# Two attentions in one kernel: the order of all steps and the choice of engines set anew

## The chip, the cores and the metric

The kernel runs on one core of a Trainium2 chip. The metric is the device time in microseconds (us) of one execution. The engines are TensorE (PE), VectorE (DVE), ScalarE (ACT), GpSimd (POOL) and SyncE (SP, which issues the DMAs here). TensorE's results land in PSUM; the other operands lie in SBUF.

## The reference

`B, H, S, D = 8, 8, 576, 64`. A first attention has two parts whose outputs are added; a mixture of four causal attention heads works on the sum.

```python
q_d = q.reshape(B, H, Sd, 4, D).mean(axis=3)          # k_d, v_d likewise; Sd = 144
out_d = sm_attn(q_d, k_d, v_d)                        # softmax attention on pooled rows
out_up = np.repeat(out_d, 4, axis=2)
mask = np.abs(pos[:, None] - pos[None, :]) < 4
out_local = softmax(np.where(mask, q @ k.T / 8, -1e9)) @ v
x = (out_up + out_local) as [B, S, H * D]

logits = x @ w_gate                                   # 4 experts, the best 2 by softmax weights
for e in range(4):
    a = causal_softmax((x @ wq[e]) @ (x @ wk[e]).T / 8)
    out += gate[e] * (a @ (x @ wv[e]) @ wo[e])
```

## The kernel before

The work is cut by batch (8) and, in the first attention, by pair of heads (4 pairs, index `c`); in the second by pair of experts (index `p`, 2) and by unit of query blocks (`u`, 1 to 4). Three stages overlap: while stage 3 of batch `b` runs, stage 2 of `b + 1` and stage 1 of `b + 2` run beside it.

- Stage 1, `s1_local`: scores of a band of 64 columns, mask (`l_mask`, L500), maximum (`l_max`, L503), subtraction (`l_sub`, L512), exponent (`l_exp`), sum (`l_sum`, L515), `l_rec`, and the norm `l_nrm` (L518). `s1_down`: q, k and v pooled by four (`qd` and `kd`; `vd`, two additions L549 and L550 on `lr` and `vd`), scores, exponent (`d_exp`), norm `d_nrm` (L591, on ACT three instructions of L589). `s1_out`: transposes, products, the sum `x` (L652), and its split into a rounded part `xh` (L657, ACT) and a rest `xl` (L658), with a short rest `xt` (L660), since the projections multiply in a rounded float32 and correct with the rest.
- Stage 2: projections `qk` and `v` (L681), a tail `vt`, the gate.
- Stage 3: `s2_scores` (L821) with mask and maximum (`s_max`, L841), exponent on ACT (`s_exp`, L844), sum (`s_eps`, L314 on POOL), reciprocal (`s_rec`, L849), and the norm `s_nrm` (L852), which multiplies the rows `pr` by reciprocal and gate weight; `s2_trans` transposes the rows (`tq`); `s2_av` multiplies with v, adds the two halves (`o_add`), and splits the result into `oh` (L942, ACT) and the rest `ol` (`o_lo`, L943); `s2_out` multiplies with `wo` and stores.

Every step is written as a call of `op(kind, engines, cost, function, ...)`. Where two engines are named, either can run it:

```python
op("s_nrm", "GV", (...), lambda g, ...: eng[g].tensor_scalar(
    rows_of[t], rows_of[t], st[:, x, 3:4], gt()[:, t, p:p + 1], op0=OP.mult, op1=OP.mult), ...)
op("o_lo", "GV", (...), lambda g: eng[g].tensor_tensor(
    ol()[:, qlo:qhi], o()[:, 0:n], oh()[:, qlo:qhi].bitcast(F32), op=OP.subtract), ...)
```

The steps are not emitted in the order in which they are written. The table `SEQ` holds one number for each: the step's index times four, plus which of its engines runs it (or, for `down`, which of two row halves comes first); -1 is a filler matmul that keeps PE busy. `schedule` reads it, and each engine runs its instructions in that order:

```python
for x in SEQ:
    o = self.ops[x // 4] if x >= 0 else self.filler()
    o.which = x % 4 if x >= 0 else 0
    o.who = o.eng[o.which]
    out.append(o)
```

An engine waits, by semaphores, for the data of its next instruction, and what stands behind that one in its queue waits too. Nothing in the program orders DVE against POOL where they share no data. The four PSUM buffers (`big`) are handed out in the order of `SEQ` as well.

Of the kernel before, what the change touches and what calls it, by code (L numbers as in the profile page):

```python
# [17 lines left out]
    24, 4, 177, 0, -1, -1, -1, -1, 136, 173, 124, 120, 140, 189, 192, 197, 144, 272, 200, -1, 232, 16, 216, 236, 149,  # L18
    268, -1, -1, -1, 284, 152, 8, 220, 240, 205, 12, 412, 208, 416, 288, 244, 376, 156, 360, 160, 214, 164, 248, 364,
    380, 180, 168, 320, 185, 293, 324, 532, 296, 384, 429, 252, 432, 568, 312, 256, 224, 504, 536, 437, 316, 388, 508,  # L20
    776, 572, 736, 228, 328, 332, 260, 300, 265, 540, 304, 708, 128, 336, 308, 392, 396, 440, 456, 340, 420, 544, 460,
    772, 816, 712, 444, 548, 400, 344, 740, 404, 584, 464, 424, 784, 840, 368, 132, 408, 468, 588, 612, 448, 592, 596,
    276, 744, 748, 28, 453, 552, 788, 600, 616, 844, 904, 604, 752, 900, 372, 348, 512, 793, 988, 609, 556, 280, 756,
    620, 472, 760, 353, 560, 357, 796, 624, 992, 476, 480, 668, 672, 32, 913, 916, 1056, 484, 764, 564, 921, 488, 37,
    812, 768, 924, 492, 500, 628, 632, 636, 640, 576, 580, 660, 20, 940, 800, 1016, 1052, 497, 804, 64, 664, 944, 644,
    648, 656, 1196, 676, 1020, 1200, 680, 1065, 684, 40, 45, 688, 876, 728, 520, 68, 652, 810, 92, 84, 48, 1172, 724,
    1068, 928, 692, 100, 720, 716, 516, 848, 1204, 1236, 696, 56, 880, 52, 1024, 61, 705, 1209, 524, 1168, 781, 104,
    528, 76, 820, 112, 948, 1073, 1076, 853, 73, 1212, 884, 952, 824, 1444, 700, 1232, 932, 888, 1028, 1244, 896, 956,
    80, 892, 1216, 1248, 960, 1081, 1508, 1084, 1221, 964, 968, 938, 1252, 856, 1032, 89, 972, 860, 1224, 1140, 1144,
    1100, 96, 864, 976, 985, 868, 1088, 1104, 1148, 732, 1440, 1280, 1036, 873, 981, 909, 828, 1284, 1504, 1152, 1320,  # L30
    1256, 1092, 1761, 1156, 1324, 1260, 1161, 1517, 1328, 1060, 1041, 1096, 1544, 1468, 1044, 1520, 1264, 1556, 1564,
    1548, 1764, 1048, 1228, 1525, 1004, 1528, 1108, 996, 1472, 1112, 1116, 1120, 1124, 1533, 1188, 1476, 1680, 1268,
    1368, 1536, 1540, 1272, 1332, 1336, 1340, 1684, 1372, 1552, 1276, 1480, 1344, 1836, 1376, 1840, 1484, 1192, 1988,
    2404, 1348, 1560, 1688, 832, 1000, 1241, 1568, 1693, 1696, 1488, 1656, 1773, 1352, 1776, 1492, 836, 1724, 1380,
    2072, 1728, 1652, 1736, 1700, 1288, 1496, 1984, 1128, 1356, 1704, 1137, 1180, 1781, 1292, 1296, 1784, 1388, 1384,
    1132, 1788, 1300, 1360, 1792, 1304, 1400, 1404, 1392, 1397, 1452, 1364, 1740, 2356, 2360, 1732, 1876, 1176, 1888,
    1500, 1828, 1832, 2068, 1008, 1448, 2080, 1184, 1880, 2084, 2012, 1592, 1308, 2016, 1596, 1012, 1408, 1412, 1416,
    2089, 2092, 2328, 2400, 1745, 1604, 1708, 1573, 1576, 1748, 2413, 1312, 1892, 1600, 2020, 1317, 2844, 1420, 1424,
    2416, 1628, 1796, 2024, 1712, 1632, 2144, 2149, 1428, 2028, 2421, 2032, 1588, 2848, 1884, 1757, 1896, 1752, 2332,
    1672, 1585, 1581, 1432, 1608, 1900, 1612, 1636, 2036, 1616, 1512, 1620, 1624, 1640, 1716, 1676, 2424, 1905, 1668,  # L40
    2429, 1844, 1908, 2364, 1437, 1664, 1644, 1720, 1848, 1852, 1800, 1648, 2368, 1804, 2136, 1912, 1856, 2097, 2040,
    1860, 2140, 1976, 1980, 1968, 2940, 1972, 1917, 2872, 2044, 2100, 2876, 1456, 2372, 2106, 1164, 1808, 1460, 2376,
    2432, 2292, 2304, 3648, 2296, 2880, 2936, 2381, 1812, 1660, 2048, 2052, 2184, 2308, 1864, 2056, 2524, 1816, 2196,
    2188, 2456, 1873, 1768, 116, 2460, 1868, 1920, 2436, 2384, 1940, 2388, 1464, 1924, 3004, 2528, 1996, 1932, 2884,
    2200, 1820, 2060, 2192, 1928, 3008, 1824, 2532, 2076, 2228, 2152, 2156, 2160, 2240, 2205, 2244, 2232, 2300, 2236,
    1992, 2976, 2108, 2464, 2112, 2116, 2000, 2164, 3012, 2168, 2469, 2120, 1944, 3016, 2208, 2172, 2249, 2620, 2409,
    1936, 1948, 1952, 2625, 3080, 2216, 2472, 2476, 2004, 2348, 2480, 2212, 2180, 2176, 2628, 2124, 2128, 2340, 2344,
    2336, 2980, 2312, 1956, 1961, 2536, 2065, 2572, 2888, 2576, 2252, 2633, 2316, 1965, 2220, 2484, 2540, 2488, 3077,
    2580, 2257, 3020, 2892, 2544, 2225, 108, 2945, 2264, 2984, 2584, 3356, 2268, 2324, 2592, 2896, 2261, 2448, 2589,
    2392, 3360, 3364, 2492, 2452, 2396, 2548, 2320, 2440, 2444, 3040, 3052, 3044, 2272, 2808, 3328, 2008, 2132, 2276,  # L50
    2280, 2820, 2552, 2949, 2952, 2764, 2776, 2812, 2957, 2556, 2768, 2504, 2988, 2284, 2960, 3433, 2508, 2512, 2900,
    2636, 2496, 2640, 2501, 2780, 2644, 2560, 2648, 2824, 2692, 2696, 3256, 3260, 3264, 2864, 3024, 3332, 2964, 3028,
    2352, 3056, 2772, 2784, 2516, 2652, 3032, 2816, 2656, 2968, 2704, 2712, 2716, 2661, 2972, 3368, 2828, 3180, 3185,
    2289, 3037, 3268, 2788, 2564, 2700, 3372, 2832, 2860, 2521, 2596, 3376, 3272, 2708, 2904, 2568, 3172, 3176, 3048,
    3380, 3277, 2600, 3429, 3441, 3444, 2612, 2604, 3672, 2664, 4036, 3676, 3088, 3188, 3449, 3192, 3092, 3384, 3388,
    3452, 3196, 3200, 3204, 3097, 3457, 3100, 3604, 3608, 2721, 2841, 3060, 3612, 3105, 3108, 3644, 2724, 3496, 3500,
    2616, 2856, 3972, 3764, 4032, 3112, 3616, 2733, 2608, 3976, 2737, 3824, 3828, 3460, 3980, 2852, 3948, 2868, 2992,
    2668, 3208, 2672, 3680, 2740, 3064, 3069, 2684, 3984, 3213, 3988, 2677, 2836, 3216, 2680, 3072, 2729, 3504, 3508,
    3085, 2744, 2800, 3684, 3620, 2748, 2792, 3760, 2797, 2908, 2804, 3464, 3220, 4076, 3944, 3336, 3688, 3708, 3992,
    4072, 3692, 2912, 3996, 3225, 2752, 3696, 3712, 3116, 2760, 4044, 3124, 2757, 3512, 3516, 4048, 3120, 3136, 3520,  # L60
    3128, 3348, 2996, 3700, 2916, 3144, 4053, 3340, 3716, 4056, 2920, 3284, 3524, 3528, 3148, 4220, 3720, 2924, 3228,
    3296, 3288, 3232, 4100, 3300, 2928, 3392, 3292, 3544, 3724, 3132, 4104, 3532, 3140, 4061, 4064, 3404, 3304, 3396,
    3236, 3344, 3548, 3832, 3552, 3704, 3308, 3896, 3240, 3556, 3436, 4452, 3000, 4225, 4068, 3153, 3836, 3536, 3156,
    3244, 4456, 3773, 3317, 3169, 4800, 3541, 3560, 3840, 3352, 3844, 2932, 3848, 3900, 3776, 3160, 3164, 3852, 3780,
    3660, 3408, 3400, 4584, 3412, 3856, 3736, 3784, 4108, 3740, 3320, 3788, 3313, 3416, 3860, 4276, 3792, 3769, 4280,
    3744, 3468, 3796, 3564, 3652, 4000, 3248, 3325, 3568, 3904, 3908, 3748, 3572, 3865, 3588, 3472, 3912, 3868, 3593,
    3421, 3752, 3576, 4004, 3424, 3916, 3920, 4268, 3756, 3476, 4272, 3480, 3924, 3928, 4136, 4424, 3952, 3964, 4156,
    3596, 3484, 4140, 3960, 4148, 3600, 4460, 3580, 3656, 4040, 4184, 3956, 3584, 4428, 4196, 4188, 4380, 4392, 4232,
    3252, 3932, 4236, 4824, 3488, 3664, 3624, 4828, 4241, 4316, 4244, 2688, 4465, 4112, 4384, 3800, 3492, 4228, 3628,
    3632, 4116, 3636, 4320, 3641, 3804, 3936, 4249, 4160, 4580, 3968, 4328, 4080, 3668, 4192, 4388, 4200, 4324, 4284,  # L70
    4832, 4836, 3941, 4252, 4288, 4593, 4292, 3808, 4840, 4468, 4120, 3817, 4296, 4844, 4849, 4796, 4332, 4088, 4008,
    4012, 4016, 4300, 4472, 4124, 4258, 4152, 4144, 5484, 4852, 4440, 4436, 4128, 3728, 4596, 4601, 4604, 4336, 4133,
    4640, 4644, 4164, 4900, 4857, 3812, 4092, 4432, 4020, 3732, 3280, 4024, 4936, 4897, 4029, 4940, 4944, 5124, 4648,
    5440, 4653, 4396, 4401, 5444, 4404, 4408, 5128, 4656, 4476, 4412, 4304, 4660, 4312, 4664, 4309, 4668, 4909, 4912,
# [1022 lines left out]
```

## Time and profile before

| what | us |
|---|---|
| timed runs: median of 3 (lowest, highest) | 473.93 (472.72, 474.66) |
| profiled execution | 469.35 |
| its span, first to last instruction | 467.6 |
| busy: PE, DVE, ACT, POOL | 444.7, 386.9, 334.5, 312.3 |
| mean granted TensorE clock | 0.996 of 2.4 GHz |

An instruction that an engine has started counts as busy until it ends, also while it stands still. The chain of work that ended last is found backwards from the last instruction: at each step the view goes to what released it, or to the instruction ahead of it on its engine. A piece's length there is the part of the instruction that lies on the chain.

### The profile page before, as it was taken

The page shows a single profiled execution, that of the slowest core. Times are in us where ns is not written, and L with a number is a line of the kernel's source. Part 1 is how long each engine was busy: PE and PEld are TensorE (multiplying, and loading weights), DVE is VectorE, ACT ScalarE, POOL GpSimd, SP SyncE. Part 2 cuts the span into 40 slices and gives each one's busy share as a digit, 9 for nine tenths or more (in the row PEclk, how much of TensorE's full clock was granted, in tenths as well). Part 3 has the DMA queues.
Part 4 walks back from the last instruction along what each step waited for, and adds up shares of the span by engine and source line. Part 5 has one row for each costly group of instructions (what it writes and reads, how often), then busy time and mean ns, then how long its engine had stood idle before and what let it go on. Part 6 is the DMA issues. An engine that isn't in the chain of part 4 may idle for free.

```text
span 467.6 us, 23426 instructions
## 1 busy us (share of the span) xinstructions
PE 444.7 (95%) x9911; PEld 403.5 (86%) x9911; DVE 386.9 (83%) x1038; ACT 334.5 (72%) x1075; POOL 312.3 (67%) x509
## 2 busy tenths in 40 slices
PE   8889899999999999999999999999979999999996
PEld 4778898888889898998889988899879898999885
DVE  7999999989989889889888799877777788457871
ACT  6978678885776857867888668673878765356874
POOL 6989798898269859467876486878784364512340
PEclk9999999999999999999999999999989999999999
DMA  8876476332435253445236331441440520011112
GB/s 254 231 221 158 98 216 175 86 98 70 136 102 175 65 151 99 131 122 181 62 102 183 109 97 39 149 117 34 141 147 3 173 70 3 3 63 53 53 55 101
DMA packets 44312, 52.90 MB, mean 113 GB/s; under 512 B 4144, under 2 KB 27184, under 8 KB 44208
## 3 DMA queue, kind: packets, MB, share of 16 engines
q1 hardware_dynamic: 44208, 51.40, 37.7%
q8 instruction: 78, 1.28, 1.2%
q14 instruction: 26, 0.21, 0.1%
HBM read 40.90 MB, written 9.44 MB: 108 GB/s over the span
## 4 chain that ended last, share of the span: by engine, by line
PE 58%; DVE 15%; POOL 4%; issue 3%; ACT 2%; DMA 1%; POOLq 0%; DVEq 0%; ACTq 0%
PE pj L681 10%; PE pv L681 9%; PE sq L821 8%; PE o L931 7%; PE po L681 6%; PE tq L365 4%; DVE pr L852 3%; PE tp L365 2%; PE sc L497 2%; PE o L632 2%; PE scd L570 2%; PE po L978 2%; DVE ol L943 1%; PE pv L733 1%; POOL pr L852 1%
## 5 line engine op out<-in xcount | busy, mean ns | idle before, releaser
L844 ACT ACTIVATE pr<-pr,pst 128x512 f32<-128x512 f32 (+8 forms) x144 | 80.0, 557 | 8.4 <-DVE pst L841 8.0
L681 PE MATMUL pj<-xh,wqk_h 64*128 64x320 f32 (+1 forms) x512 | 80.5, 309 | 0.0
L681 PE MATMUL pj<-xh,wqk_l 64*128 64x320 f32 (+1 forms) x512 | 76.2, 292 | 0.5 <-issue 0.5
L681 PE MATMUL pj<-xl,wqk_h 64*128 64x320 f32 (+1 forms) x512 | 76.1, 292 | 0.0
L841 DVE CUSTOM_DVE_ANT_0 pr<-sq,causal_t 128x448 f32<-128x448 f32 (+8 forms) x144 | 64.3, 483 | 7.5 <-PE sq L821 6.6
L852 POOL TENSOR_SCALAR pr<-pr,pst,gt 128x64 f32<-128x64 f32 (+8 forms) x78 | 54.8, 709 | 20.4 <-DVE pst L849 12.2
L821 PE MATMUL sq<-k,q 64*64 64x256 f32 (+6 forms) x768 | 53.5, 372 | 2.9 <-DVE vg L309 1.1
L681 PEld LDWEIGHTS pj<-xh,wqk_h 64*128 64x128 f32 x512 | 48.9, 186 | 1.7 <-issue 0.9
L681 PEld LDWEIGHTS pj<-xh,wqk_l 64*128 64x128 f32 x512 | 48.9, 186 | 0.8 <-issue 0.8
L681 PEld LDWEIGHTS pj<-xl,wqk_h 64*128 64x128 f32 x512 | 48.7, 185 | 0.0
L681 PE MATMUL pv<-wvg_h,xh 64*128 64x260 f32 x256 | 39.9, 300 | 2.5 <-issue 2.5
L821 PEld LDWEIGHTS sq<-k,q 64*64 64x64 f32 x768 | 31.4, 133 | 11.2 <-DVE vg L309 1.3
L852 DVE TENSOR_SCALAR pr<-pr,pst,gt 128x192 f32<-128x192 f32 (+8 forms) x66 | 39.2, 604 | 1.0
L681 PE MATMUL pv<-wvg_l,xh 64*128 64x260 f32 x256 | 37.9, 285 | 0.5 <-DVE wvg_l L443 0.5
L580 ACT ACTIVATE dp<-scd,dst 128x144 f32<-128x144 f32 x96 | 35.3, 377 | 4.0 <-PE tp L365 1.7
L681 PE MATMUL pv<-wvg_h,xl 64*128 64x260 f32 x256 | 37.7, 283 | 0.0
L365 PE MATMUL tq<-ident,pr 64*128 64x64 f32 x736 | 33.7, 224 | 3.2 <-DVE pst L316 0.7
L518 POOL TENSOR_TENSOR lp<-lp,lst 128x640 f32<-128x640 f32 x24 | 31.5, 1314 | 7.2 <-DVE lst L517 5.6
L307 ACT COPY ptb<-tq 128x384 f32<-128x384 f32 (+4 forms) x70 | 30.9, 491 | 7.5 <-PE tq L365 7.3
L681 PE MATMUL po<-oh,wo_h 64*128 64x256 f32 x224 | 35.4, 307 | 0.0
L365 PEld LDWEIGHTS tq<-ident,pr 64*128 64x128 f32 x736 | 29.6, 138 | 5.8 <-issue 1.9
L658 POOL TENSOR_TENSOR xl<-x,xh 128x576 fp32r<-128x576 f32 x21 | 30.2, 1438 | 6.2 <-ACT xh L657 6.2
(180 smaller groups left out, 1470.1 us busy)
## 6 DMA issues: line engine op xcount, KB each, us to landing
lv<-in_v_dram SPq DMA_DIRECT2D x64, 160.0 KB, 4.0
lk<-in_kT_dram SPq DMA_DIRECT2D x32, 292.0 KB, 4.0
lq<-in_qT_dram SPq DMA_DIRECT2D x32, 292.0 KB, 4.3
out_dram<-ot SPq DMA_DIRECT2D x28, 288.0 KB, 2.8
lr<-in_v_dram SPq DMA_DIRECT2D x28, 256.0 KB, 3.5
lr<-in_v_dram SPq DMA_DIRECT2D x56, 32.0 KB, 3.2
wst<-in_wqk_dram SPq DMA_DIRECT2D x1, 1024.0 KB, 7.8
vx<-vg SPq DMA_DIRECT2D x8, 128.0 KB, 3.0
```

Source lines behind the costliest of these rows:

```text
L307: A.copy(dst, src)
L365: T.transpose(ps()[:, 512 * x + z[x]:512 * x + z[x] + 64], data[r, 0:128], ident[r, r])
L497: T.matmul(sc()[halves[h ^ (t // 5)], 512 * (t // 5) + W * i:512 * (t // 5) + W * i + W], q()[r, z:z + 64], k()[r, z:z + W], start=True, s ...
L518: op("l_nrm", "GV", (pool_tt(n), dve(n)), lambda e: eng[e].tensor_tensor(p(), p(), st[:, :, 2:3].to_broadcast([128, NT, W]), op=OP.mult), ...
L580: A.activation(p()[:, t, :], scs()[:, at * t:at * t + SD], AF.Exp, bias=st[:, t, 4:5], scale=1.0 / 128.0, accum_out=st[:, t, 0:1])
L658: op("xl", "GV", (1360, dve(576)), lambda e: eng[e].tensor_tensor(xl(), x(), xh()[:, 0:S].bitcast(F32), op=OP.subtract), r=[x, (xh, 0)], w ...
L681: mine = T.matmul(parts(z), w(i, z)[r], m(i, z)[r], start=c == 0 and phase == 0 and i == 0, stop=c == n - 1 and phase == 1 and i == 2)
L821: T.matmul(pss[x][0]()[halves[e ^ turned(t)], at_of[x] + at + to:at_of[x] + at + to + n1 - n0], q()[r, 64 * t:64 * t + 64], k()[r, n0:n1], ...
L841: op("s_max", "V", dve(n) + 4, lambda x=x, t=t, n=n, src=src: V.tensor_tensor_reduce(rows_of[t], src(), causal_t[:, S - 64:S + 256] if t = ...
L844: op("s_exp", "A", 281 + n / 1.2, lambda x=x, t=t, n=n: A.activation(rows_of[t], rows_of[t], AF.Exp, bias=st[:, x, 4:5], scale=-1.0, accum ...
L852: op("s_nrm", "GV", (327 + n / 1.2 + max(0, n - 384) * 1.1, 189 + n / 1.92), lambda g, x=x, t=t, n=n: eng[g].tensor_scalar(rows_of[t], row ...
L931: T.matmul(obs[x]()[r, q0:q1], vg()[kr, j, 64 * (2 * p + e):64 * (2 * p + e) + 64], pt()[kr, e, j, q0:q1], start=j == 0, stop=j == len(job ...
```

## The change

Only `SEQ` changes: 2540 steps in another order, 2550 numbers in place of 2548 (ten fillers, eight before), and for the steps that two engines can run, other choices. The planner that made the new table lets an instruction of DVE and one of POOL that want the same way into SBUF run one after the other in its plan; the planner is not part of the program, and no semaphore is added for it. All costs, buffers, tiles and functions are those of before. The table takes one line more, so a line below it has a number higher by one after the change: L852 becomes L853.

```diff
 SEQ = (
-    24, 4, 177, 0, -1, -1, -1, -1, 136, 173, 124, 120, 140, 189, 192, 197, 144, 272, 200, -1, 232, 16, 216, 236, 149,
...
+    4, 177, 24, 0, -1, -1, -1, -1, 136, 173, 188, 16, 120, 140, 124, 192, 144, 149, 197, 268, 8, 12, 200, 204, 152,
...
```

Choices of engine, number of steps before and after (`vd` is two instructions a step, `d_nrm` on ACT three):

| step | DVE | POOL | ACT |
|---|---|---|---|
| `s_nrm` | 66, 47 | 78, 97 | |
| `o_lo` | 14, 10 | 18, 22 | |
| `vd` | 11, 8 | 17, 20 | |
| `xt` | 15, 12 | 17, 20 | |
| `xl` | 11, 12 | 21, 20 | |
| `l_nrm` | 8, 15 | 24, 17 | |
| `l_sub` | 6, 10 | 14, 10 | |
| `d_nrm` | 6, 4 | 18, 8 | 8, 20 |
| `qd` | 7, 13 | 25, 19 | |
| `kd` | 6, 8 | 26, 24 | |
| `wlo` | 5, 4 | 5, 6 | |
| `d_scl` | 5, 11 | | 27, 21 |

The rest (sums, copies out of PSUM) move by at most three steps each.

The first place is DVE's queue near 382 us of the profile before, where the second half of batch 5's stage 3 ends (`ol` and `pr` are of batch 5, `lr` and `vd` of batch 7). Before:

```order
L943 TENSOR_TENSOR ol<-oc,oh 128x256
L849 RECIPROCAL pst_79<-pst_79 128x2
L852 TENSOR_SCALAR pr_132<-pr_132,pst_79,gt 128x448
L852 TENSOR_SCALAR pr_128<-pr_128,pst_79,gt 128x384
L549 TENSOR_TENSOR lr_95<-lr_95 128x2x256
L550 TENSOR_TENSOR vd<-lr_95 128x256
L309 COPY ptb<-tq 128x2x3x64 x2
L309 COPY ptb<-tq 128x2x64
```

The same place after the change, behind the maxima of the same unit:

```order
L842 ISA pr_131,pst_75<-sq,causal_t 128x64
L842 ISA pst_75 128x1
L550 TENSOR_TENSOR lr_96<-lr_96 128x2x256
L551 TENSOR_TENSOR vd<-lr_96 128x256
L853 TENSOR_SCALAR pr_130<-pr_130,pst_80,gt 128x576
L310 COPY pt<-tp 128x580
L310 COPY ptb<-tq 128x2x5x64
L310 COPY ptb<-tq 128x2x4x64
```

`ol` and the norms of 448 and 384 columns have left for POOL; one pair of `lr` and `vd` and one norm stay, and copies follow.

POOL's queue at the same place, from the norm of 512 columns of that batch to the rest `xl` of batch 7. Before:

```order
L852 TENSOR_SCALAR pr_129<-pr_129,pst_80,gt 128x512
L658 TENSOR_TENSOR xl<-x,xh 128x576
L549 TENSOR_TENSOR lr_96<-lr_96 128x2x256
L550 TENSOR_TENSOR vd<-lr_96 128x256
L943 TENSOR_TENSOR ol<-oc,oh 128x320
L660 TENSOR_TENSOR xh<-x,xh 128x64 x2
L658 TENSOR_TENSOR xl<-x,xh 128x576
L852 TENSOR_SCALAR pr_131<-pr_131,pst_75,gt 128x64
L660 TENSOR_TENSOR xh<-x,xh 128x64
```

After:

```order
L853 TENSOR_SCALAR pr_132<-pr_132,pst_78,gt 128x320
L853 TENSOR_SCALAR pr_129<-pr_129,pst_80,gt 128x512
L944 TENSOR_TENSOR ol<-oc,oh 128x256
L853 TENSOR_SCALAR pr_132<-pr_132,pst_79,gt 128x448
L754 TENSOR_TENSOR cm<-gw_91,gs 128x5x4
L659 TENSOR_TENSOR xl<-x,xh 128x576
L661 TENSOR_TENSOR xh<-x,xh 128x64
L944 TENSOR_TENSOR ol<-oc,oh 128x256
L661 TENSOR_TENSOR xh<-x,xh 128x64
L853 TENSOR_SCALAR pr_131<-pr_131,pst_75,gt 128x64
```

The norm of 448 columns and an `ol` that DVE had now stand behind the norm of 512 columns and ahead of `xl`, with a step of the gate; the pair `lr` and `vd` and the second `xl` have left this piece of the queue (that `xl` runs on DVE).

The second place is DVE's queue near 276 to 282 us, batch 3's second pair of experts (`lp` and `dp` belong to stage 1 of batches 6 and 5). Before:

```order
L852 TENSOR_SCALAR pr_130<-pr_130,pst_76,gt 128x576
L777 TENSOR_REDUCE gs<-gw_91 128x5
L778 RECIPROCAL gs<-gs 128x5
L852 TENSOR_SCALAR pr_132<-pr_132,pst_75,gt 128x448
L591 TENSOR_TENSOR dp<-dp,dst_88 128x432
L852 TENSOR_SCALAR pr_128<-pr_128,pst_75,gt 128x384
L316 TENSOR_REDUCE pst_77<-pst_77 128x3
L943 TENSOR_TENSOR ol<-oc,oh 128x256
L309 COPY ptb<-tq 128x2x3x64 x2
L309 COPY ptb<-tq 128x2x64
```

After:

```order
L850 RECIPROCAL pst_75<-pst_75 128x2
L944 TENSOR_TENSOR ol<-oc,oh 128x256
L853 TENSOR_SCALAR pr_127<-pr_127,pst_80,gt 128x256
L504 TENSOR_REDUCE lst_70<-lp 128x10
L853 TENSOR_SCALAR pr_132<-pr_132,pst_75,gt 128x448
L513 TENSOR_TENSOR lp<-lp,lst_70 128x640
L310 COPY ptb<-tq 128x2x5x64
L516 TENSOR_REDUCE lst_69<-lp 128x10
L317 TENSOR_REDUCE lst_69<-lst_69 128x10
```

Three norms, the norm of `dp` and the `ol` stood in a row but for two short sums; now `ol`, two norms and a subtraction of `lp` (L513) stand there, with a maximum between them, and copies follow.

## Rows read from the trace of the kernel before

**Rows 1.** The page: span, and busy us, share, instructions of the engines.

```profile
span 467.6 us, 23426 instructions
...
PE 444.7 (95%) x9911; PEld 403.5 (86%) x9911; DVE 386.9 (83%) x1038; ACT 334.5 (72%) x1075; POOL 312.3 (67%) x509
```

**Rows 2.** The page: shares of the last chain, by engine and by line.

```profile
PE 58%; DVE 15%; POOL 4%; issue 3%; ACT 2%; DMA 1%; POOLq 0%; DVEq 0%; ACTq 0%
PE pj L681 10%; PE pv L681 9%; PE sq L821 8%; PE o L931 7%; PE po L681 6%; PE tq L365 4%; DVE pr L852 3%; PE tp L365 2%; PE sc L497 2%; PE o L632 2%; PE scd L570 2%; PE po L978 2%; DVE ol L943 1%; PE pv L733 1%; POOL pr L852 1%
```

**Rows 3.** Windows: sum over 104:119, 129:151, 276:288 and 374:391.

```profile
sum 66.00, PE 61.98 PEld 57.95 DVE 61.70 ACT 44.03 POOL 48.48; mean PE 15.50 PEld 14.49 DVE 15.43 ACT 11.01 POOL 12.12
```

**Rows 4.** Timeline of DVE, 144 to 149 us: start, duration, then the instruction.

```profile
144.51 0.87 DVE L658 TENSOR_TENSOR xl<-x,xh 128x576 fp32r<-128x576 f32 x1
...
145.97 1.42 DVE L852 TENSOR_SCALAR pr<-pr,pst,gt 128x192 f32<-128x192 f32 x1
```

**Rows 5.** Timelines of POOL, 144 to 149 and 382 to 389 us.

```profile
144.75 1.27 POOL L852 TENSOR_SCALAR pr<-pr,pst,gt 128x512 f32<-128x512 f32 x1
145.99 1.28 POOL L512 TENSOR_TENSOR lp<-lp,lst 128x640 f32<-128x640 f32 x1
...
383.20 0.77 POOL L852 TENSOR_SCALAR pr<-pr,pst,gt 128x512 f32<-128x512 f32 x1
```

**Rows 6.** Timelines of DVE at 248, 345 and 356 us: the same forms undisturbed.

```profile
248.32 0.33 DVE L852 TENSOR_SCALAR pr<-pr,pst,gt 128x192 f32<-128x192 f32 x1
...
345.15 0.41 DVE L943 TENSOR_TENSOR ol<-oc,oh 128x256 fp32r<-128x256 f32 x1
...
345.56 0.47 DVE L943 TENSOR_TENSOR ol<-oc,oh 128x320 fp32r<-128x320 f32 x1
...
356.62 0.51 DVE L852 TENSOR_SCALAR pr<-pr,pst,gt 128x448 f32<-128x448 f32 x1
```

**Rows 7.** Chain in order of time: start us, us on the chain, what.

```profile
84.26 0.93 DVE pr L852
...
107.28 1.65 DVE ol L943
...
131.58 1.35 DVE ol L943
...
146.05 1.34 DVE pr L852
...
175.47 1.29 POOL lr L549
...
182.94 1.64 POOL xl L658
...
279.94 1.35 DVE ol L943
...
283.76 1.28 DVE ol L943
...
384.13 1.58 DVE pr L852
...
387.43 0.84 DVE vd L550
```

**Rows 8.** The page's groups: busy us, mean ns, idle before, for norms.

```profile
L852 POOL TENSOR_SCALAR pr<-pr,pst,gt 128x64 f32<-128x64 f32 (+8 forms) x78 | 54.8, 709 | 20.4 <-DVE pst L849 12.2
...
L852 DVE TENSOR_SCALAR pr<-pr,pst,gt 128x192 f32<-128x192 f32 (+8 forms) x66 | 39.2, 604 | 1.0
...
L518 POOL TENSOR_TENSOR lp<-lp,lst 128x640 f32<-128x640 f32 x24 | 31.5, 1314 | 7.2 <-DVE lst L517 5.6
```

**Rows 9.** Groups by form on ACT: the norm of the pooled attention.

```profile
L589 ACT ACTIVATE dp<-dp,dst 128x144 f32<-128x144 f32 x24 | 8.2, 407 | 1.2 <-DVE dst L584 1.2
```

**Rows 10.** Waits: total us, times, longest us.

```profile
POOL pst L314 <- ACT pr L844: 38.6, 14, 12.1
...
PE pv L681 <- issue: 2.5, 1, 2.5
```

263 rows, old and new, of the table SEQ are left out of this document.

## The prediction, made before the run

> **What bounds the kernel now.** I read the page first: the busy shares [rows 1]. TensorE (PE) is busy for 444.7 of 467.6 us, so at most 22.9 us of the span has PE idle. VectorE (DVE) has 386.9 and GpSimd (POOL) 312.3. The profiled execution took 469.35 us, 1.75 more than its span, and 1% less than the median of the timed runs (473.93): I work against 469.35 and scale at the end.
>
> Next the chain that ended last [rows 2]. The view follows it back to 83 us. Of the whole span PE has 58% of it, DVE 15% (70 us), POOL 4% (19 us), ACT 2%. So PE sets the pace, and in places DVE does. Those places are four stretches, together 66 us, in which the chain runs mostly over DVE (104 to 119, 129 to 151, 276 to 288, 374 to 391). The windows of them [rows 3] show DVE busy for 61.70 of 66 us and PE for 61.98. There 4.0 us of PE idle could be closed; the other 18.9 of the 22.9 no row ties to DVE.
>
> What is DVE busy with? Look at the timeline from 144 to 149 us on both engines [rows 4, 5]. The norm `pr` at 145.97 (192 columns) takes 1.42 us. On POOL a 640-column addition runs from 145.99 to 147.27, and the DVE norm ends just after it. The same form undisturbed takes 0.33 us at 248.32 [rows 6]. The other way round, POOL's 512-column norm at 144.75 takes 1.27 us beside DVE's `xl` at 144.51, and 0.77 at 383.20. So one engine's instruction stands still while the other's runs, and the standing counts as busy. In the whole trace this shows on DVE only in instructions that read two tensors from SBUF (`xl`, `ol`, `lr`, `vd`, ...) and in the norms L852; the maxima, sums and copies from PSUM keep their length beside POOL. The Trainium skill, "SBUF — State Buffer", section "Who interferes with whom", says this in its own way: the port pair the two share is an exclusive lock. The trace agrees (1.42 against 0.33).
>
> How much of it is on the path? I took each DVE and POOL piece of the chain and subtracted the form's quiet duration. Six pieces [rows 7]: 107.28 (1.65 - 0.47), 131.58 (1.35 - 0.47), 146.05 (1.34 - 0.33), 279.94 (1.35 - 0.41), 283.76 (1.28 - 0.41) and 384.13 (384 columns, 1.58 less at most the 0.51 of 448), the quiet ones from [rows 6]. That is 1.18 + 0.88 + 1.01 + 0.94 + 0.87 + 1.07 = 6.0 us. Nineteen smaller pieces, the first at 84.26 and the last at 387.43 [rows 7], give 8.5 by the same subtraction. **14.5 us of standing lie on the chain.**
>
> **The change part by part.** Nothing is computed differently; 2540 planned steps get another order, some another engine, and the head gets ten filler matmuls instead of eight.
>
> (1) *Fewer instructions on DVE that can be made to stand.* Counted in the built orders: norms 66 to 47, `o_lo` 14 to 10, the two additions of `vd` 22 to 16, `xt` 15 to 12, against `l_nrm` 8 to 15, `l_sub` 6 to 10, `xl` 11 to 12, and three small kinds: 161 to 138, 14% fewer. At an unchanged wait each, that takes 14% of 14.5 = 2.1 us from the chain. This is the small end.
>
> (2) *Those that stay are placed anew.* In the two fences of orders above, DVE's run of five locking instructions (`ol`, two norms, `lr`, `vd`) near 384 us is down to `lr`, `vd` and one norm, and the run near 280 us is broken up by a maximum and copies. Of the 14.5 us, 7.0 belong to steps that go to POOL (at 84, 107, 283 and 384 us among them) and the rest to steps that stay (131, 146, 280). The large end is all 14.5. Between 2.1 and 14.5 I take half, 7: nothing in the program enforces the exclusion, no wait is added, and an engine that runs half a microsecond off its plan meets the other one again, since POOL is busy two thirds of the time.
>
> (3) *What is late next.* PE. Of 7 us less on DVE only what PE stood idle can come out: 4.0 us in the four stretches [rows 3]. From the other 18.9 I take 1, since DVE also stands before 83 us, where the chain isn't followed. So **-5 us**.
>
> (4) *ACT gets more:* twelve `d_nrm`, three instructions of 407 ns each [rows 9], 14.6 us, less a few scalings and copies. ACT is busy for 334.5 us and holds 2% of the chain [rows 1, 2], so I cost it at nothing; the cover is ACT's idle time. If a fifth of it came ahead of a copy for which PE waits it would cost 3 us. For a gain by it I see no reason, as POOL, which it relieves, holds 4%.
>
> (5) *POOL* gets 19 norms more (709 ns each, 13.5 us) and loses seven `l_nrm` (1314 ns, 9.2 us) [rows 8], four `l_sub` and ten `d_nrm`; I take its load as unchanged, only its order changes. It issues no DMA. Its queue is in order, and its longest wait is one at the head: `s_eps` for ACT's exponent, 38.6 us in 14 times, up to 12.1 [rows 10]; what is queued behind, norms above all, waits with it. `s_eps` stays there 30 times (31 before). Cost between -2 and +3 us; I take 0, as the count hardly moves.
>
> (6) *SP's queue* keeps its 259 steps in another order; DMA has 1% of the chain [rows 2]. The weights `wo` are loaded later (32nd of the steps before, 54th after), but their first use is in the third stage of batch 0, behind its scores. Nothing, with ±1 us. The fillers run while PE waits for the first vectors: nothing.
>
> (7) *The stall of PE at 342.7 us*, 2.5 us in which the profile shows nothing it waited for [rows 10], belongs to no part of the order; I keep it. If it is absent, 2.5 us go.
>
> Sum: 469.35 - 5 = 464.35. The ratio, 0.9893, on the median 473.93 gives **468.9 us**.
>
> **The rivals.** *A. The port is serial anyway.* Moving work between two engines that exclude each other wins nothing; only (1) is left: -2.1, and POOL's longer instructions take one of it back: 468 of 469.35, 472.6 us. For it: DVE norms average 604 ns, POOL's 709 [rows 8], and 43 norms leave DVE for POOL while 24 come. The Trainium skill, "Perfetto Trace Analysis", section "Optimizing Scalar/DVE Operations", warns that offloading between those two might not help. By that rule the time would be this one; the trace shows the serial running (rows above), but also that it costs nothing off the chain. Against it: much of the standing is on DVE where the chain is. The planner's exclusion not holding on the chip ends here too.
>
> *B. Slower: POOL takes DVE's place on the chain.* The place is the one of the second fence: between 374 and 391 us POOL now has `ol` and the norms ahead of the `xl` that the last batch's projections need. Price: norms and `ol` are some 18 us of the chain (3% and 1%) [rows 2], of which some 8 are quiet work (18 less 11 of standing, by the subtraction above); if two thirds go to POOL at 1.5 times the length (0.77 for 512 columns, 0.51 for 448 on DVE) that is +2.7, no wait is saved since POOL stands too, and half of one mean wait at its head (38.6/14 = 2.8) adds 1.4: +4, 473.4 of 469.35, or 478.0 us. It decides once POOL's share of the chain passes DVE's. Against it: from 163 to 187 us the chain already runs over POOL (at 175.47 and 182.94, [rows 7]), and POOL has over 150 us idle in all.
>
> *C. All of it.* The exclusion holds: 14.5 us, and PE packs closer: 454.9, or 459.3 us. Against it: PE's idle in the stretches is 4 us; the rest must come out elsewhere.
>
> **How the numbers follow.** Forecast (about 0.5 to 2% faster) 0.46; C 0.12; A, no change, 0.20; B 0.22. A measurement of this kernel tells about 0.5% from no change. So faster 0.58, same 0.20, slower 0.22. The range reaches to C's and B's times, 459.5 to 478: outside lie a better C and a worse B, under 0.2 together. The forecast's own range is 464.5 to 471.5.
>
> **What would show it.** Right: the mean of DVE's norms L853 falls from 604 ns towards 450; `ol` and `vd` on DVE no longer exceed 1.3 us; DVE's busy time falls below 370; its share of the chain falls and PE's rises; PE's idle falls from 22.9 to about 18 us. A: DVE's and POOL's means as before, PE idle the same. B: POOL's share of the chain above 10%, waits of PE's transposes for POOL norms. Wrong in another way: ACT's share well above 2% with `d_nrm` in it, or new waits of PE for a load.

## The result, and the profile after

| kernel | median, us (lowest, highest) | ratio to before (95% interval) |
|---|---|---|
| before, same chip | 473.33 (469.10, 474.66) | |
| after | 459.58 (458.47, 461.50) | 0.9729 (0.9658 to 0.9800) |

The change is 13.75 us faster; 468.9 was predicted. The profiled execution of after took 461.5 us, 7.85 less than the profiled 469.35 of before: that one was among the quickest of its kernel. Run a second time the two gave 473.49 and 459.24 us (ratios 1.0013 and 0.9736). The ratios leave out executions more than 1.5% above the fastest of their kernel, while the medians keep them (one of the six of b_nolock_2, 465.39 us), and the second profiled execution of before, 476.96 us, was such a one and stands in no table here.

The page of after, as [rows 1, 2] of before: span, busy us, the last chain by engine and by line.

```profile
span 459.7 us, 23436 instructions
...
PE 442.0 (96%) x9913; PEld 404.2 (88%) x9913; DVE 373.3 (81%) x1024; ACT 342.3 (74%) x1111; POOL 296.1 (64%) x503
...
PE 76%; DVE 12%; DMA 4%; ACT 3%; issue 2%; SPq 1%; POOL 0%; ACTq 0%; DVEq 0%
PE pj L682 16%; PE po L682 10%; PE sq L822 9%; PE o L932 8%; PE pv L682 8%; PE tq L366 5%; PE tp L366 4%; PE sc L498 3%; PE o L633 3%; PE scd L571 2%; PE po L979 2%; PE pv L556 1%; DVE lst L504 1%; PE pv L734 1%; PE o L640 1%
```

PE has 76% of the span and DVE 12, but 58 and 15 before cannot be set beside them as they stand: that chain was followed over 83% of its span only, this one over 98%. Of the part that was followed, PE had 70% and DVE 18 before, and 78 and 12 after. No norm nor `ol` is left among these lines. DVE is busy for 13.6 us less, POOL for 16.2 less. PE is idle for 17.7 us (459.7 - 442.0; before 22.9), and its busy time fell too, by 2.7.

Groups of after (busy us, mean ns, idle before), as [rows 8]; the last line is POOL's norms.

```profile
L853 DVE TENSOR_SCALAR pr<-pr,pst,gt 128x256 f32<-128x256 f32 (+8 forms) x47 | 24.8, 544 | 0.4
...
L944 DVE TENSOR_TENSOR ol<-oc,oh 128x320 fp32r<-128x320 f32 (+1 forms) x10 | 4.8, 483 | 1.5 <-ACT oh L943 1.4
...
L551 DVE TENSOR_TENSOR vd<-lr 128x256 f32<-128x256 f32 x8 | 5.5, 684 | 0.3
...
L853 POOL TENSOR_SCALAR pr<-pr,pst,gt 128x448 f32<-128x448 f32 (+8 forms) x97 | 65.2, 679 | 34.5 <-DVE pst L850 24.9
```

DVE's norms fell from 604 to 544 ns, POOL's from 709 to 679. DVE's `ol` takes 483 ns a piece, near its quiet length (0.41 and 0.47 in [rows 6]). Adding up, over all forms, what each instruction takes above the shortest tenth of its form: DVE's standing fell from 45.8 to 25.0 us, POOL's from 26.4 to 21.2.

### The profile page after: what moved, and what is told of

Same layout as the page of the kernel before. It is cut to its first block, busy times and chain, and to the rows that moved or that the text cites. A ratio compares the mean times of both kernels' runs of the same rounds, so it can differ in the third digit from the quotient of the medians.

```text
span 459.7 us, 23436 instructions
## 1 busy us (share of the span) xinstructions
PE 442.0 (96%) x9913; PEld 404.2 (88%) x9913; DVE 373.3 (81%) x1024; ACT 342.3 (74%) x1111; POOL 296.1 (64%) x503
## 3 DMA queue, kind: packets, MB, share of 16 engines
q8 instruction: 78, 1.28, 1.2%
## 4 chain that ended last, share of the span: by engine, by line
PE 76%; DVE 12%; DMA 4%; ACT 3%; issue 2%; SPq 1%; POOL 0%; ACTq 0%; DVEq 0%
PE pj L682 16%; PE po L682 10%; PE sq L822 9%; PE o L932 8%; PE pv L682 8%; PE tq L366 5%; PE tp L366 4%; PE sc L498 3%; PE o L633 3%; PE scd L571 2%; PE po L979 2%; PE pv L556 1%; DVE lst L504 1%; PE pv L734 1%; PE o L640 1%
## 5 line engine op out<-in xcount | busy, mean ns | idle before, releaser
L853 POOL TENSOR_SCALAR pr<-pr,pst,gt 128x448 f32<-128x448 f32 (+8 forms) x97 | 65.2, 679 | 34.5 <-DVE pst L850 24.9
L845 ACT ACTIVATE pr<-pr,pst 128x64 f32<-128x64 f32 (+8 forms) x144 | 80.2, 559 | 7.3 <-DVE pst L842 7.3
L682 PE MATMUL pj<-xh,wqk_h 64*128 64x320 f32 (+1 forms) x512 | 81.8, 309 | 0.1
L842 DVE CUSTOM_DVE_ANT_0 pr<-sq,causal_t 128x192 f32<-128x192 f32 (+8 forms) x144 | 64.5, 483 | 5.2 <-PE sq L822 4.1
L822 PE MATMUL sq<-k,q 64*64 64x64 f32 (+6 forms) x768 | 52.2, 371 | 0.7 <-DVE pd L310 0.6
L682 PE MATMUL pv<-wvg_h,xh 64*128 64x260 f32 x256 | 38.6, 292 | 0.0
L682 PE MATMUL po<-oh,wo_l 64*128 64x256 f32 x224 | 33.6, 292 | 0.0
L682 PE MATMUL po<-ol,wo_h 64*128 64x256 f32 x224 | 33.6, 291 | 0.0
L519 POOL TENSOR_TENSOR lp<-lp,lst 128x640 f32<-128x640 f32 x17 | 23.1, 1359 | 16.3 <-DVE lst L518 14.6
L659 POOL TENSOR_TENSOR xl<-x,xh 128x576 fp32r<-128x576 f32 x20 | 28.6, 1430 | 6.9 <-ACT xh L658 6.9
```

Source lines behind the costliest of these rows:

```text
L519: op("l_nrm", "GV", (pool_tt(n), dve(n)), lambda e: eng[e].tensor_tensor(p(), p(), st[:, :, 2:3].to_broadcast([128, NT, W]), op=OP.mult), ...
L659: op("xl", "GV", (1360, dve(576)), lambda e: eng[e].tensor_tensor(xl(), x(), xh()[:, 0:S].bitcast(F32), op=OP.subtract), r=[x, (xh, 0)], w ...
L682: mine = T.matmul(parts(z), w(i, z)[r], m(i, z)[r], start=c == 0 and phase == 0 and i == 0, stop=c == n - 1 and phase == 1 and i == 2)
L822: T.matmul(pss[x][0]()[halves[e ^ turned(t)], at_of[x] + at + to:at_of[x] + at + to + n1 - n0], q()[r, 64 * t:64 * t + 64], k()[r, n0:n1], ...
L842: op("s_max", "V", dve(n) + 4, lambda x=x, t=t, n=n, src=src: V.tensor_tensor_reduce(rows_of[t], src(), causal_t[:, S - 64:S + 256] if t = ...
L845: op("s_exp", "A", 281 + n / 1.2, lambda x=x, t=t, n=n: A.activation(rows_of[t], rows_of[t], AF.Exp, bias=st[:, x, 4:5], scale=-1.0, accum ...
```

## Where the time went, by stretch

Four stretches of each profiled execution, cut at three points of PE: the first product of the projections `qk` of batch 1, of the second pair of experts of batch 5 ("5b"), and of batch 6. In us, one execution each; the experiments follow below.

| kernel | start to 1 | 1 to 5b | 5b to 6 | 6 to end | span |
|---|---|---|---|---|---|
| before | 78.6 | 245.1 | 47.2 | 96.7 | 467.6 |
| b_few | 82.4 | 247.0 | 47.5 | 95.8 | 472.6 |
| b_nl_norms | 81.8 | 244.1 | 49.1 | 95.7 | 470.7 |
| b_nl_ol | 83.0 | 243.1 | 47.4 | 95.7 | 469.2 |
| b_nl_two | 77.1 | 241.0 | 45.9 | 95.6 | 459.4 |
| b_nolock | 77.7 | 236.8 | 46.0 | 95.5 | 456.0 |
| b_nolock_2 | 77.4 | 238.7 | 48.7 | 95.6 | 460.4 |
| after | 80.2 | 241.8 | 42.5 | 95.1 | 459.7 |
| after_again | 80.4 | 237.9 | 42.5 | 95.2 | 456.1 |
| a_nolock | 77.3 | 239.9 | 42.3 | 95.0 | 454.6 |
| a_nolock_2 | 76.1 | 240.1 | 42.3 | 95.0 | 453.5 |
| bo_ac | 94.7 | 271.3 | 46.4 | 104.5 | 516.9 |
| ao_bc | 87.9 | 265.2 | 47.1 | 99.7 | 499.9 |

## The experiments

**1. No standing at all, in both orders.** Every DVE instruction that can be made to stand (161 before, 138 after) copies one of its inputs instead: a maximum over an added axis of length 1. The values of those steps are left out; order, choices and sizes stay. The copies of two-input steps take about what the steps take undisturbed (`vd` 420 ns against 425, `lr` 677 against 665 to 693). Those of the norms fit less well: 192 columns 334 against 330, but 576 columns 733 against some 560; over the 66 norms a copy takes 466 ns on average, some 36 more than the shortest tenths of the same widths (430).

```diff
+    def one(dst, src):
+        V.tensor_reduce(dst, strided1(src), op=OP.max, axis=AX.X)
...
-        op("xt", "GV", (260, dve(64)), lambda e: eng[e].tensor_tensor(
+        op("xt", "GV", (260, dve(64)), lambda e: one(xh()[:, S:S + 64], xh()[:, S - 64:S].bitcast(F32)) if e == "V" else eng[e].tensor_tensor(
```

> The kernel before, its order and choices of engines untouched, but each of DVE's 161 instructions that were seen to stand (two inputs from SBUF, and the norms) is replaced by a reduction over an axis of length one, which reads one tensor from SBUF and takes about as long; it copies, so what these steps compute is left out. Theory 1 (the gain is the standing that went away): DVE's busy time falls by about 40 us, POOL's by about 20, and the time falls to 0.965 to 0.98 of before, about what the change gives. Theory 2 (the new order is better for other reasons, the standing was beside other work): 0.99 to 1.00. The prediction's own term was 7 of 14.5 us, 0.985.

> The changed kernel with the same replacement (138 instructions of DVE). Theory 1: little is left to win, 0.96 to 0.97 of before, under 1% below the changed kernel. Theory 2: equal to the changed kernel within 0.5%, and well below the kernel before with the same replacement. If it stands over 2% below the changed kernel, the change has left much of the standing on the path.

Measured, beside 472.39 us of before: b_nolock 460.04 us, ratio 0.9733 (0.9670 to 0.9797); a_nolock 455.75 us, 0.9656 (0.9561 to 0.9751). So standing cost before 12.35 us, and after some 3.8 (459.58 - 455.75; the two ran beside different executions of before, and their intervals overlap). Both ratios lie in the ranges of Theory 1, though DVE's busy time fell by 33 us and not by 40. Between the two orders without standing 4.3 us were left, as Theory 2 has it for the whole gain, with intervals that overlap; both ran again beside each other (experiment 6).

The pages of b_nolock and of a_nolock_2: busy us, and the chain by engine.

```profile
PE 438.7 (96%) x9911; PEld 401.4 (88%) x9911; DVE 354.0 (78%) x1038; ACT 333.2 (73%) x1075; POOL 288.5 (63%) x509
...
PE 90%; DMA 5%; issue 2%; ACT 1%; SPq 1%; DVE 0%; DVEq 0%
```

```profile
PE 439.4 (97%) x9913; PEld 402.5 (89%) x9913; DVE 357.6 (79%) x1024; ACT 341.6 (75%) x1111; POOL 277.4 (61%) x503
...
PE 86%; DMA 4%; DVE 4%; ACT 3%; issue 2%; SPq 0%; POOL 0%; DVEq 0%; ACTq 0%
```

Only DVE's instructions were edited, and POOL's busy time fell too, from 312.3 to 288.5 us: its standing goes from 26.4 to 2.3. That is the lock of [rows 4, 5] seen from the other engine. The Trainium skill, "SBUF — State Buffer", section "Who interferes with whom", has the pair exclude each other; the trace agrees, with these 24 us.

**2. Order and choices apart.** Before's order with after's choices, and the reverse; 332 numbers of the table get another last digit (the order of row halves in `down`, in which 19 steps differ, stays with the order of steps), the first ones of bo_ac being:

```diff
-205, 185, 293
+204, 184, 292
```

> The order of the kernel before with the engine choices of the changed one. Theory 1a (the choices carry the gain, since fewer instructions of DVE can be made to stand, 138 in place of 161): 0.975 to 0.985 of before. Theory 1b (the order carries it, by placing them apart): 0.995 to 1.01. If order and choices only work together it is slower than before, 1.01 to 1.03.

> The order of the changed kernel with the engine choices of the kernel before. Theory 1a: 0.995 to 1.01 of before. Theory 1b: 0.975 to 0.985. If order and choices only work together: 1.01 to 1.03.

Measured: bo_ac 518.64 us, ratio 1.1006 (1.0924 to 1.1087); ao_bc 500.12 us, 1.0585 (1.0511 to 1.0659). Both are slower than either kernel, and by far more than the 1.01 to 1.03 forecast for that case, though bo_ac has the smaller number of instructions that can stand. The chain of bo_ac by engine, and PE's two longest waits (total us, times, longest us):

```profile
PE 50%; DVE 20%; POOL 14%; issue 8%; ACT 6%; DMA 1%; SPq 0%; POOLq 0%; DVEq 0%; ACTq 0%
...
PE tp L372 <- POOL lp L525: 6.7, 3, 4.3
PE tq L372 <- POOL pr L859: 3.9, 7, 1.2
```

POOL's share is 14% and PE's transposes wait for POOL's norms (`lp` L525, `pr` L859). What a choice is worth depends on what stands ahead of it in that engine's queue; it has no price of its own.

**3. Eleven standing steps of the chain moved.** Before, with three `o_lo`, seven norms and one `vd`, which hold 7.0 us of the chain's standing, given from DVE to POOL at their places.

```diff
-1757, 1585, 2065, 1965, 2737, 4529, 5865, 5893, 8085, 8521, 8365
+1756, 1584, 2064, 1964, 2736, 4528, 5864, 5892, 8084, 8520, 8364
```

> The order of before; only eleven steps change their engine, from DVE to POOL, those whose standing was on the chain (7.0 us in the trace of before) and which the change has moved to POOL too: three o_lo, seven norms, one vd. The prediction's step (2) counts their 7.0 us as leaving the path: 0.985 to 0.995 of before. If choices only work with an order made for them, it is 1.00 to 1.02: the steps wait in POOL's queue instead.

Measured: 473.19 us, ratio 1.0009 (0.9973 to 1.0045). Busy us and chain by engine:

```profile
PE 444.6 (94%) x9911; PEld 405.5 (86%) x9911; DVE 375.9 (80%) x1026; ACT 334.8 (71%) x1075; POOL 318.9 (67%) x521
...
PE 75%; DVE 10%; DMA 6%; issue 3%; POOL 2%; ACT 2%; SPq 1%; DVEq 0%
```

The range of step (2), 0.985 to 0.995, is missed. DVE is busy for 11 us less and holds 10% of the chain instead of 18 (of the part that was followed), and the time is the same: other standing steps (`vd`, `lp`, `xh`) are late in their stead, and the chain that ended last runs over loads for 6%. The Trainium skill, "Perfetto Trace Analysis", section "Optimizing Scalar/DVE Operations", warns that offloading between these two may not help; the run agrees (1.0009).

**4. The norms alone.** Before, with only the 66 norms of DVE copying as in experiment 1.

```diff
-            op("s_nrm", "GV", ..., lambda g, ...: eng[g].tensor_scalar(
+            op("s_nrm", "GV", ..., lambda g, ...: one(rows_of[t], rows_of[t]) if g == "V" else eng[g].tensor_scalar(
```

> Before with the one-input replacement for the 66 norms on DVE alone (the norms there are left out, it copies). All 161 replaced gave 0.973. The norms' share of the standing on the chain was 6.5 of 14.5 us (ol 4.7): if that share holds, 0.985 to 0.99. If they are nearly all of it, 0.975; if nothing, 1.00.

Measured: 472.44 us, ratio 0.9980 (0.9943 to 1.0016). The mean of those instructions fell from 604 to 467 ns, 9 us in all, for at most 0.6% of the time: of the three forecasts "nothing" is the nearest. As the copies are longer than undisturbed norms (466 ns against 430), what the norms' standing costs may be somewhat more.

**5. The other 95, and `ol` alone.** Before, with the instructions that read two tensors from SBUF copying and the norms left as they are (b_nl_two); then only the 14 `o_lo` of DVE (b_nl_ol).

```diff
-        op("o_lo", "GV", (pool_tt(n), dve(n)), lambda g: eng[g].tensor_tensor(
+        op("o_lo", "GV", (pool_tt(n), dve(n)), lambda g: one(ol()[:, qlo:qhi], oh()[:, qlo:qhi].bitcast(F32)) if g == "V" else eng[g].tensor_tensor(
```

> Left out: the order and choices of before, but the 95 instructions of DVE that read two tensors from SBUF (o_lo, vd, xl, xt, l_nrm, l_sub, d_nrm, v_add, wlo) copy one of them instead; the 66 norms on DVE still compute. All 161 replaced took 12.35 us off (472.39 to 460.04), the 66 norms alone 0.2 percent. Theory 1 (the cost of standing sits in the instructions with two inputs, which are on the chain more often): 460 to 462.5 us, ratio 0.974 to 0.979. Theory 2 (the parts pay only together: with either kind left, the next meeting takes the time back): 466 to 471 us, ratio 0.985 to 0.996. Rival (neither kind matters and the copies win by something else than standing): no difference between kinds by count, 95 of 161 of the gain, 7 us, 465.5 us.

> Left out: the order and choices of before, but the 14 subtractions o_lo on DVE (the rest ol of stage 3) copy one of their inputs; the other 81 two-input instructions and the norms still compute. Replacing all 95 two-input instructions took 10.9 us off (472.86 to 461.98). By the chain of before, ol has 4.7 of its 14.5 us of standing, the most of any step. Theory 1 (a step's cost is its standing on the chain): a third of 10.9, some 3.5 us, 469 to 470 us, ratio 0.991 to 0.994. Theory 2 (ol is the last step ahead of PE's products of a unit, so it carries the larger part): 462 to 466 us, ratio 0.977 to 0.986. Rival (the time sits in the two-input steps of stage 1, ahead of the next batches' projections; ol only shows on the chain): 472 to 473.5 us, ratio 0.998 to 1.001.

Measured: b_nl_two 461.98 us, ratio 0.9790 (0.9746 to 0.9835); b_nl_ol 470.65 us, 0.9946 (0.9905 to 0.9988). Theory 1 holds for the first: by the medians the two-input instructions carry 10.9 of the 11.3 us that all 161 cost beside them on the same chip (b_nolock_2 of experiment 6), by the ratios 2.1 of 2.5%. `ol` carries some 2.6 us (0.54%), nearest to Theory 1, though under its forecast third, and with an interval that reaches into the rival's range (0.998). Groups of b_nl_two (busy us, mean ns, idle before):

```profile
L873 DVE TENSOR_SCALAR pr<-pr,pst,gt 128x192 f32<-128x192 f32 (+8 forms) x66 | 39.3, 605 | 1.0
...
L314 DVE TENSOR_REDUCE ol<-oh 128x320 fp32r<-128x320 f32 (+1 forms) x14 | 6.1, 442 | 1.1 <-ACT oh L963 1.0
...
L314 DVE TENSOR_REDUCE vd<-lr 128x256 f32<-128x256 f32 x11 | 4.6, 420 | 0.4
```

The norms stand as before (605 ns), and 5.5 us of their standing lie on the chain of b_nl_two by the same subtraction; yet taking them away as well is worth 0.5 us by the medians and 1.9 by the ratios (0.9790 and 0.9749), within the noise. Standing that the chain shows is not always standing that costs.

**6. The two orders without standing, beside each other.** The kernels of experiment 1 again; there is no edit beyond that one.

> The same kernel as in a_nolock (the order and choices of after, its 138 instructions of DVE that can be made to stand replaced by copies), beside the next one, to settle what is left between the two orders when DVE never stands. Theory 1 (the new order is better in itself by some 4 us): 455 to 456.5 us, ratio 0.963 to 0.966, below b_nolock_2 by over 2.5 us. Theory 2 (all of the change's gain is standing put off the path): the same as b_nolock_2 within 1.5 us, 457 to 459.5.

> The same kernel as in b_nolock (the order and choices of before, its 161 instructions of DVE that can be made to stand replaced by copies), beside the one ahead. Theory 1: 459 to 461 us again, ratio 0.971 to 0.976. Theory 2: within 1.5 us of the one ahead.

Measured, beside 472.86: a_nolock_2 455.57 us, ratio 0.9650 (0.9602 to 0.9698); b_nolock_2 461.52 us, 0.9749 (0.9689 to 0.9810). The two differ by 5.95 us by the medians and by 4.7 by the ratios; the intervals just touch, but the first pair gave 4.3 the same way. In the table above the place is plain: between the projections of batch 5's second pair and batch 6, every profile of the old order with its choices takes 45.9 to 49.1 us, standing or not, and every one of the new 42.3 to 42.5. Theory 1 holds, with the median of b_nolock_2 half a microsecond above its range and the ratio inside: this part of the gain is there without the lock. Neither the order nor the choices alone bring it: bo_ac needs 46.4 us for this stretch and ao_bc 47.1, though with waits of their own in it (the longest 1.7 and 1.4 us).

What happens there? PE's work is the same (1012 and 1013 matmuls). Windows over that stretch, of before and then of after; columns are length, busy us (instructions) of PE, PEld, DVE, ACT and POOL, granted clock, DMA share, GB/s:

```profile
323.70:370.90 47.20, 44.54 (x1012) 40.14 (x1010) 34.98 (x94) 35.82 (x123) 29.96 (x51) 0.96 0.37 111
```

```profile
322.10:364.60 42.50, 42.46 (x1013) 39.41 (x1010) 35.98 (x104) 35.11 (x125) 31.60 (x53) 1.00 0.41 122
```

Inside it, of before and then of after:

```profile
334.00:340.00 6.00, 6.00 (x183) 4.88 (x178) 5.52 (x13) 5.56 (x23) 3.02 (x5) 1.00 0.92 281
340.00:345.00 5.00, 2.68 (x116) 2.36 (x107) 4.96 (x18) 4.74 (x19) 3.90 (x8) 0.96 0.75 245
345.00:348.00 3.00, 2.82 (x26) 2.82 (x28) 2.26 (x9) 2.36 (x9) 1.99 (x4) 0.50 0.26 69
```

```profile
334.00:340.00 6.00, 6.00 (x198) 4.99 (x196) 5.81 (x23) 5.33 (x18) 4.12 (x6) 1.00 0.44 117
340.00:346.00 6.00, 5.96 (x104) 5.62 (x98) 5.86 (x16) 5.93 (x28) 4.93 (x10) 1.00 0.49 151
```

Before has a burst of loads and stores here (0.92 of the DMA engines' time), then the stall of 2.5 us of [rows 10], then 3 us at a granted clock of 0.50, the 1.2 GHz level. The lower clock follows the stall in before, b_nl_norms and b_nolock_2 alone; in the other four profiles of the old order the clock stays at 1.00 in this stretch. After moves about as much in the whole stretch (111 and 122 GB/s) and spreads it (0.44 and 0.49); PE doesn't stop and the clock stays at 1.00. PE's waits in this stretch in b_nolock_2 (total us, times, longest us):

```profile
PE pv L702 <- issue: 2.5, 1, 2.5
PE sq L842 <- DVE ot L324: 1.4, 1, 1.4
```

The second one is PE behind a copy of `ot` on DVE, which itself waits, on the chain, for the store of the tile before (4.9 us). After has neither wait in its stretch.

## Why the prediction was right in sign and short in size

**Step (1), the count.** It gave 2.1 us for 14% fewer instructions, as if the choices could be priced without the order. Experiment 2 rules that out: the new choices in the old order cost 46 us. The count was no lower bound but no measure at all.

**Step (2), the standing on the chain.** The mechanism is the one named, and the size was near: 14.5 us on the chain against 12.35 and 11.3 measured (this is in part luck, as the pieces were not the ones that cost); "half", 7 us, against some 8 that went (12.35 less 3.8). By the table, the cost of standing sat in two stretches of the old order: some 4.6 us up to batch 1's projections (median 82.1 with the two-input steps standing, 77.5 without; single executions, and those with standing spread from 78.6 to 83.0) and some 7 from there to 5b (244.6, 237.8). The new order pays nothing in the second (239.9, 240.0) and 3.6 in the first. But the pieces were the wrong ones. The norms, some 6.5 us of the chain's standing, cost some 1 us (0.2%, by the interval at most 0.6%); the steps of the fences near 384 us cost next to nothing (6 to end: 95.7 with and 95.6 without standing); and the head, into which the chain wasn't followed, carries a third.

**Step (3), what is late next, failed.** It capped the gain at the 5 us that PE stood idle beside DVE. In the profiled pair PE's idle time did fall by 5.2 us, but that execution of before was a quick one: in b_few, b_nl_norms and b_nl_ol, at 0.995 to 1.001 of before, PE is idle for 25.9 to 28.0 us and not 22.9, and in after_again for 14.7. So there was more idle time to close than this trace showed. Nor is PE's busy time a floor: it fell by 2.7 us in the change, and by 6.0 in b_nolock with PE's program untouched. A matmul at the lower clock counts as busy for longer (a `pv` product near 347 us of before 0.42 us, one near 348.5, at the full clock, 0.28); what else the 6.0 us are was not traced.

**Steps (6) and (7) failed, and hold the larger miss.** The stall at 342.7 us was said to belong to no part of the order and was kept, and SP's queue was costed at nothing. The stall is in all seven profiles of the old order with its choices (0.5 to 2.5 us, ahead of the same products `pv`) and in none of the four of the new. (The new order has one of this kind of its own, at 193 to 199 us, of 0.4 us in after and after_again and of 1.6 and 1.3 in the two without standing.) The stretch is worth 4.9 us (median 47.4 against 42.5), over a third of the gain. In before the stall, the lower clock behind it (in 345 to 348 us 26 matmuls at the pace of half the clock, some 1.3 us) and the wait behind `ot` (0.2 us here, 1.4 in b_nolock_2) make up 4.0 of its 4.7. Which of the burst, SP's order or PE's own is the cause was not tried apart.

**Steps (4) and (5).** ACT's 7.8 us more cost nothing to be seen: its share of the chain went from 2 to 3%. (The copies out of PSUM moved by more than the three steps that the description of the change gives: seven `pta` went from DVE to ACT and four `pt` came the other way.) POOL's load was taken as unchanged; it fell by 16.2 us, 5.2 of it standing, and POOL is off the chain (0%).

**The scale.** The sum was made against an execution 0.8% quicker than the medians since. It differs from the other profiles with two-input standing in the first stretch alone (78.6 against 81.8 to 83.0); so the profiled executions, at a ratio of 0.9833, show less of the gain than the medians, at 0.9729.

**The signs.** `ol` below 1.3 us, PE's idle time near 18 (17.7), DVE's share down and PE's up: as said, the idle time with what step (3) says of that execution. DVE's norms came to 544 ns, not toward 450; one `vd` still took 1.40 us; DVE's busy time is 373, not under 370. More standing is left than forecast; it has left the places that matter.

**The rivals.** A falls with the sign, though it describes b_few. B is what bo_ac does (POOL at 14% of the chain, waits for its norms), so its mechanism is real once the order isn't planned with the choices. C gave 459.3 us, within 0.3 of the measured, for another reason: it had all 14.5 us of standing go, where 8 did and 5 came from the stretch of batch 5. So the time lies at the low end of the range (459.5 to 478.0), 0.1 us inside it, while executions of after spread over 3 us: that it lies inside is luck. The forecast's own range, 464.5 to 471.5, misses it.

## What to carry to other kernels

Cost a contended port by replacing the suspected instructions with one-input copies of the same length, and compare the lengths: it prices the whole effect at once, where the chain of one execution names pieces that turn out to be worth little, and moving eleven such pieces by themselves gained nothing. Don't cap a gain by the bound engine's idle time in one execution, and don't set a stall aside because the profile names no releaser: see which loads run there. An order and its engine choices have one price together.

## What the runs showed of the hardware

The stall that the profile calls "issue" goes with PE's own instructions. One DMA queue carries them, by the page of before (packets, MB, share of the engines):

```profile
q8 instruction: 78, 1.28, 1.2%
```

1.28 MB over 19,822 matmuls and weight loads is some 64 bytes each, so that queue must be PE's, in 78 blocks of 16 KB (16,384 bytes in the trace), 256 instructions each. When the block beside the stall landed, and when PE went on, in the trace of each profile of the old order (us):

| kernel | block lands | PE goes on | between | stall |
|---|---|---|---|---|
| before | 343.75 | 345.19 | 1.4 | 2.5 |
| b_few | 349.27 | 350.67 | 1.4 | 1.4 |
| b_nl_norms | 345.93 | 347.37 | 1.4 | 2.3 |
| b_nl_ol | 345.88 | 347.21 | 1.3 | 2.1 |
| b_nl_two | 336.32 | 337.51 | 1.2 | 0.5 |
| b_nolock | 333.31 | 334.79 | 1.5 | 1.3 |
| b_nolock_2 | 336.27 | 337.69 | 1.4 | 2.5 |

Seven times PE goes on 1.2 to 1.5 us after the landing, whatever the stall's length. Ahead of it PE runs short matmuls, nearly all of the first attention, 116 and their 107 weight loads in 2.7 us, while data fill the DMA engines. That fits PE running out of instructions while its next block shares the engines with the burst.

The place bears out the first half. Number PE's matmuls, weight loads and waits in the trace, from 0 at the start: in all seven the stalled product has number 15,554, or 15,553. In the thirteen traces of the table of stretches, PE has 76 waits of over 0.3 us for which the view names nothing but "issue"; 71 of them stand at numbers that differ by whole multiples of 256, to within one, a block's length, each 1.2 to 1.7 us after a landing. Of the 195 waits for which it names a releaser, two do. So PE stood at the end of a block and waited for the next.

The second half stays a reading, as no run changed the burst alone. In the 6 us up to the landing the DMA engines are busy for 0.90 to 0.96 of the time in the seven profiles of the old order. In the four of the new they are for 0.41 to 0.45; there PE passes the same number, 1.3 to 1.5 us after the landing too, without a wait. But ao_bc, with 0.39, still waits 0.4 us there (the view puts it down to a step of DVE). The Trainium skill, "Runtime: NRT & Kernel Launch", section "Instruction fetch mechanics", has the blocks of this size, which the trace shows too, and calls their cost mostly hidden; at this place it was not (0.5 to 2.5 us).
